# Decay attention and a gated feed-forward: more of the first batch in float32 on TensorE, and unit scales from shared parts

## The chip, the cores and the metric

The kernel runs on one core of one Trainium2 chip. The time is the device time of one execution, in microseconds (us), median over several executions. A core has five engines that run their own queues of instructions: TensorE (PE in the profile, with its weight loads as PEld), VectorE (DVE), ScalarE (ACT), GpSimd (POOL) and SyncE (SP), which here issues every DMA. An instruction waits for semaphores of other engines at the head of its own queue.

## The reference

Attention with a running decay over 8 batches of 8 heads (576 positions, 64 channels), then a feed-forward block over the 4608 tokens:

```python
scores = scale * np.matmul(q, k.transpose(0, 1, 3, 2))
cum = np.cumsum(np.log(np.clip(f, 0.0001, 1.0)), axis=-1)
decay = cum[:, :, :, None] - cum[:, :, None, :]
scores = np.where(causal, -1000000000.0, scores + decay)
attn = np.exp(scores - np.max(scores, axis=-1, keepdims=True))
attn = attn / (np.sum(attn, axis=-1, keepdims=True) + 1e-09)
x = np.matmul(attn, v)            # heads are then joined to 512 channels for each token
h = x @ w_in                      # 512 -> 2048
g = np.where(h >= 1, h, np.where(h <= -1, 0.0, (h + 1) ** 2 / 4.0))
out = g @ w_out                   # 2048 -> 512
```

Everything is float32 in and out.

## The kernel before, in words

**Attention jobs.** A job is one pair of heads of one batch. A batch is four jobs; the first batch is cut in two by rows (CUTS, L29), so jobs 0 to 3 hold its query rows 0 to 255 and jobs 4 to 7 its rows 256 to 575. There are 36 jobs, and jobs 8 to 35 are the batches 1 to 7. A job goes by row blocks r of 128 query rows (0 and 1 in jobs 0 to 3; 2, 3 and 4 in jobs 4 to 7; the last block has 64 rows, and both heads share its partitions). For each block `scores` makes q·k on PE and the decay and mask on POOL (L487, L491), into a buffer of a ring; `weights` takes the row maximum on DVE (L570), the exponential and its sum on ACT (L574), and turns the block so that keys lie on partitions. Then one matmul group per job multiplies with v, and two instructions write the result as two float16 parts, high and low, into the batch's buffer `xs[b]`.

**Two ways to turn.** Jobs below NPE (5) stay in float32: ACT scales an identity by 1/sum (L501), PE multiplies each 128x128 block by it, which turns and divides it at once (L512, L518), ACT copies the turned blocks out of PSUM (L523), and the product with v is a float32 matmul (`early_values`, L543). From job NPE on, each block is split into a high and a low float16 part (ACT L588, DVE L594), the parts are turned by DMA (L600, L603), v is split likewise (L446, L447), and the product is three float16 matmuls (`values`, L614). For jobs 6 and 7 POOL_LOW (L34) gives the low part of blocks 2 and 4 to POOL (L592), after one more ACT pass (L591). The float32 way borrows the `pr` buffers as extra score buffers and for the scaled identities: its ring has 8 score buffers, the other way's has 4.

**Weights of the feed-forward.** w_in and w_out come in 16 loads of 1 MB (L197), two to a block. Each raw load sits in a place that other data needs later (RAW, L42): slots of the weight tile itself, a spare buffer, or `xs[1]`, the buffer of batch 1's attention output. `weight_split` rounds and splits a load on DVE (L206, L209, L212), takes norms (ACT L216, PE L128), and makes the two float16 parts (ACT L221; POOL L223 and L226 for w_in, DVE L228 for w_out). CONVERT (L38) says which jobs the eight blocks are put beside.

**Units.** A unit is 256 tokens by one weight block: 24 or 48 matmuls into PSUM tile `ph` (L656; two such buffers, also used by L512 and L518), two ACT and one DVE instruction for the gate (L665, L666, L667), two for its float16 parts (L669, L670), and 12 matmuls into `po` (L684). There are 144. Those of the first 256 tokens run in three weight groups (EARLY, L36), as the weights come in. A unit needs scales: `moe_scales` makes them in 14 DVE instructions (L287 to L312), once for each of the three early groups, then once a batch, 11 times in all.

**Order.** The code lists the work in the order above, but the launch (L846) lets the framework order each engine's queue by a simulated timeline, so the order on the chip differs from that of the text.

Of the kernel before, what the change touches and what calls it, by code (L numbers as in the profile page):

```python
# [8 lines left out]
F32 = mybir.dt.float32  # L9
F16 = mybir.dt.float16  # L10
I32 = mybir.dt.int32
AF = mybir.ActivationFunctionType
ALU = mybir.AluOpType
AX = mybir.AxisListType

P = 128
EVEN_EXP = 0x7F000000
HALF_BIAS = 0x1FC00000
LOW = 2.0 ** -40
HIGH = 2.0 ** 60  # L20
MASKED = -3.0e38
# [6 lines left out]

CUTS = {0: ((0, 2), (2, 5))}  # L29

NPE = 5
NQK = 12

POOL_LOW = {6: (2, 4), 7: (2, 4)}  # L34

EARLY = ((0, 0, 3), (0, 3, 6), (0, 6, 8))  # L36

# [8 lines left out]
def kernel(  # L46
# [100 lines left out]
    def decay_sums():  # L147
        fl = early
        nb = B * H
        nc.sync.dma_start(fl[0:nb, 0:S], f.rearrange("b h s -> (b h) s"))  # L150
# [123 lines left out]
    early_z = const.tile([P, 5, NB], F32, name="early_z")  # L274

    class Scales:
        pass

    def moe_scales(b, first=0, last=NB - 1, early_group=False):
# [5 lines left out]
        w = early_z[:, :, blocks] if early_group else tiny.tile([P, 5, NB], F32, name="z")  # L285
        z.t, z.h, z.u, z.r, z.o = (w[:, i] for i in range(5))
        nc.vector.tensor_scalar(out=z.t, in0=sw[:, 0, blocks], scalar1=sv[:, b:b + 1], scalar2=None, op0=ALU.mult)  # L287
# [6 lines left out]
        nc.vector.reciprocal(z.u, z.h)
        nc.vector.tensor_scalar(out=z.u, in0=z.u, scalar1=0.5, scalar2=None, op0=ALU.mult)
        nc.vector.tensor_scalar(out=z.h, in0=z.h, scalar1=0.5, scalar2=None, op0=ALU.mult)
        gm = tiny.tile([P, 1], F32, name="gm", bufs=2)
        sm = tiny.tile([P, 1], F32, name="sm", bufs=2)
        nc.vector.tensor_reduce(out=gm, in_=mp[:, 0, blocks], axis=AX.X, op=ALU.max)
        nc.vector.tensor_reduce(out=sm, in_=mp[:, 1, blocks], axis=AX.X, op=ALU.max)  # L300
        nc.vector.tensor_scalar(
            out=gm, in0=gm, scalar1=mv[:, b:b + 1], scalar2=OVER * 1.001 * DM ** 0.5, op0=ALU.mult, op1=ALU.mult
        )
        nc.vector.tensor_scalar(out=gm, in0=gm, scalar1=1.0, scalar2=None, op0=ALU.max)
        even_pow2(gm, gm)
        z.osc = z.o[:, 0:1]
        nc.vector.tensor_scalar(
            out=z.osc, in0=gm, scalar1=sm, scalar2=4.0 / PSC, op0=ALU.mult, op1=ALU.mult
        )
        nc.vector.tensor_tensor(out=z.r, in0=z.t, in1=sw[:, 1, blocks], op=ALU.mult)  # L310
        nc.vector.tensor_scalar(out=z.r, in0=z.r, scalar1=z.osc, scalar2=None, op0=ALU.mult)
        nc.vector.reciprocal(z.r, z.r)  # L312
        return z


# [240 lines left out]
    def weights(w, r):  # L556

        if r == w.r0:
            w.pT = one.tile([P, NT5, 2, 2, S], F16, name="pT")
        nh = 2 if r < LAST else 1  # L560
        wid = min(P * (r + 1), S)
        sds = w.sds[r]
        if w.p >= NPE:
            pr = one.tile([P, PRN[r]], F16, name=f"pr{r}")
            pr = pr.rearrange("p (t l h e) -> p t l h e", t=r + 1, l=2, h=nh)
        nm = tiny.tile([P, 2], F32, name="nm", bufs=8)
        sm = tiny.tile([P, 2], F32, name="sm2", bufs=8)
        for i, (sd, sp) in enumerate(sds):
            a = sd[:, 0:wid]
            nc.vector.tensor_tensor_reduce(  # L570
                out=a, in0=sp[:, 0:wid], in1=a, scale=w.nalpha, scalar=BIG, op0=ALU.add, op1=ALU.min,
                accum_out=nm[:, i:i + 1],
            )
            nc.scalar.activation(a, a, AF.Exp, bias=nm[:, i:i + 1], scale=-1.0, accum_out=sm[:, i:i + 1])  # L574
        rc = tiny.tile([P, 2], F32, name="rc", bufs=8)
        if w.p < NPE:
            nc.vector.tensor_scalar(out=rc[:, 0:nh], in0=sm[:, 0:nh], scalar1=1e-9, scalar2=None, op0=ALU.add)
            nc.vector.reciprocal(rc[:, 0:nh], rc[:, 0:nh])
            turn_rows(w, r, [sd for sd, sp in sds], rc, diags[turn[2] % len(diags)])
            turn[2] += 1  # L580
            return
        nc.vector.tensor_scalar(
            out=rc[:, 0:nh], in0=sm[:, 0:nh], scalar1=1e-9, scalar2=1.0 / PSC, op0=ALU.add, op1=ALU.mult
        )
        nc.vector.reciprocal(rc[:, 0:nh], rc[:, 0:nh])  # L585
        for i, (sd, sp) in enumerate(sds):
            a = sd[:, 0:(r + 1) * P].rearrange("p (t e) -> p t e", e=P)
            nc.scalar.activation(pr[:, :, 0, i, :], a, AF.Copy, scale=rc[:, i:i + 1])  # L588
            mode = POOL_LOW.get(w.p, ())
            if r in mode:  # L590
                nc.scalar.activation(a, a, AF.Copy, scale=rc[:, i:i + 1])  # L591
                nc.gpsimd.tensor_tensor(out=pr[:, :, 1, i, :], in0=a, in1=pr[:, :, 0, i, :], op=ALU.subtract)  # L592
            else:
                nc.vector.scalar_tensor_tensor(  # L594
                    out=pr[:, :, 1, i, :], in0=a, scalar=rc[:, i:i + 1], in1=pr[:, :, 0, i, :],
                    op0=ALU.mult, op1=ALU.subtract,
                )
# [253 lines left out]
```

## Time and profile before

| | |
|---|---|
| median of 3 runs | 1129.2 us (1126.28 to 1130.91) |
| the profiled execution: its time, and its span from first to last instruction | 1127.8 us, 1126.0 us |
| mean granted TensorE clock | 0.956 |
| busy: DVE, ACT, POOL | 803.2 us (71%), 787.8 us (70%), 427.5 us (38%) |
| DMA: mean rate, packets under 512 B | 135 GB/s, 383968 of 408281 |

Busy times of the engines overlap: they don't add up to the span. A share over the whole span mixes three stages. Up to about 300 us the weights come in and the first two batches start; then attention jobs and units run side by side; from about 960 us on only units are left.

### The profile page before, as it was taken

The numbers are of one execution on the slowest core, as the hardware profiler recorded it, in microseconds if no ns is written. First come the engines' busy times: TensorE is split into PE (matmuls) and PEld (weight loads), VectorE is DVE, ScalarE is ACT, GpSimd is POOL, SyncE is SP. The second block draws the span as 40 slices with busy tenths as digits, with TensorE's granted clock in tenths as the row PEclk, the third lists the DMA queues.
The fourth block names the chain that finished last, engine by engine and source line by source line (L and its number), as shares of the span: only waits on it lengthen the run. The fifth ranks groups of instructions, "written<-read, shape, count | busy, mean of one in ns | idle before, by whom it ended". The sixth has DMA issues, their size and how long they took to land.

```text
span 1126.0 us, 24406 instructions
## 1 busy us (share of the span) xinstructions
PE 1020.5 (91%) x8809; PEld 662.4 (59%) x8809; DVE 803.2 (71%) x2102; ACT 787.8 (70%) x1638; POOL 427.5 (38%) x679
## 2 busy tenths in 40 slices
PE   4656667799799999999999999999999999999998
PEld 3433434556566666666766666666665666677665
DVE  5769989879788887877667668787888887332222
ACT  4567776768877887787677767787878887443443
POOL 4466775424563544444223324444444452000000
PEclk9758888899999999999999999999999999999999
DMA  7967876657886656565543656566676552300000
GB/s 221 288 177 199 225 205 176 149 126 174 202 164 156 156 132 159 140 149 149 112 100 78 155 115 153 142 151 138 161 142 149 122 123 60 78 20 2 19 20 19
DMA packets 408281, 152.18 MB, mean 135 GB/s; under 512 B 383968, under 2 KB 384992, under 8 KB 408160
## 3 DMA queue, kind: packets, MB, share of 16 engines
q1 hardware_dynamic: 408160, 150.63, 56.4%
q8 instruction: 69, 1.13, 0.4%
q14 instruction: 52, 0.43, 0.1%
HBM read 75.64 MB, written 9.58 MB: 76 GB/s over the span
## 4 chain that ended last, share of the span: by engine, by line
PE 34%; ACT 15%; DVE 7%; DMA 3%; SPq 3%; issue 2%; ACTq 0%; DVEq 0%
PE po L684 15%; PE ph L656 15%; ACT sdr L574 4%; DMA qk<-in_k_dram 3%; ACT pr L588 2%; SPq L349 2%; ACT g L669 2%; PE s L614 2%; ACT u L666 2%; PE s L481 2%; DVE qs L415 2%; ACT u L665 1%; DVE u L667 1%; DVE pr L594 1%; ACT bits L396 1%
## 5 line engine op out<-in xcount | busy, mean ns | idle before, releaser
L656 PE MATMUL ph<-x,place 128*128 128x256 f16 (+3 forms) x4608 | 417.9, 249 | 19.3 <-DVE u L667 16.5
L684 PE MATMUL po<-place,g 128*128 128x512 f16 x1728 | 404.8, 383 | 7.9 <-ACT g L669 6.7
L656 PEld LDWEIGHTS <-place 128*128 128x128 f16 x4608 | 355.7, 99 | 82.0 <-issue 33.9
L684 PEld LDWEIGHTS <-g 128*128 128x128 f16 x1728 | 167.2, 100 | 184.5 <-ACT g L669 9.2
L487 POOL TENSOR_SCALAR sdr<-ck,nsig,cqs 128x128 f32<-128x128 f32 (+1 forms) x192 | 157.1, 822 | 163.5 <-DVE pr L594 152.4
L667 DVE SCALAR_TENSOR_TENSOR u<-ph,z,u 128x512 f32<-128x512 f32 x136 | 101.7, 748 | 117.4 <-ACT u L666 115.4
L574 ACT ACTIVATE sdr<-sdr,nm 128x384 f32<-128x384 f32 (+1 forms) x248 | 137.2, 554 | 50.4 <-DVE nm L570 47.1
L665 ACT ACTIVATE u<-ph,z 128x512 f32<-128x512 f32 x136 | 104.3, 767 | 83.9 <-PE ph L656 83.8
L481 PE MATMUL s<-qkT 64*64 64x512 f16 (+11 forms) x1056 | 119.9, 341 | 33.8 <-DVE nm L570 20.8
L594 DVE SCALAR_TENSOR_TENSOR pr<-sdr,rc,pr 128x384 f16<-128x384 f32 (+2 forms) x232 | 132.6, 605 | 21.3 <-ACT pr L588 19.7
L670 DVE SCALAR_TENSOR_TENSOR g<-u,z,g 128x512 f16<-128x512 f32 x136 | 105.0, 772 | 53.4 <-ACT g L669 52.8
L669 ACT ACTIVATE g<-u,z 128x512 f16<-128x512 f32 x136 | 97.3, 716 | 62.9 <-DVE u L667 62.9
L487 POOL TENSOR_SCALAR sd<-ck,nsig,cqs 64x576 f32<-64x576 f32 x48 | 44.1, 919 | 235.8 <-issue 141.3
L588 ACT ACTIVATE pr<-sdr,rc 128x384 f16<-128x384 f32 (+1 forms) x236 | 119.1, 554 | 6.0 <-DVE rc L585 2.3
L570 DVE CUSTOM_DVE_ANT_0 sdr<-s,sdr,nalpha 128x128 f32<-128x128 f32 (+1 forms) x192 | 97.2, 545 | 19.0 <-POOL sdr L491 11.8
L491 POOL TENSOR_SCALAR_AFFINE_SELECT sdr<-sdr 128x128 f32<-128x128 f32 x248 | 88.9, 369 | 9.9
L666 ACT ACTIVATE u<-u 128x512 f32<-128x512 f32 x144 | 89.7, 623 | 2.3
L614 PE MATMUL s<-pT,vs 128*64 128x320 f16 (+3 forms) x1098 | 71.5, 282 | 7.2 <-DMA pT<-pr 6.0
L487 POOL TENSOR_SCALAR sdr<-ck,cq 128x384 f32<-128x384 f32 (+3 forms) x56 | 45.5, 813 | 65.5 <-DVE pr L594 28.1
L614 PEld LDWEIGHTS <-vs 128*64 128x64 f16 x1098 | 49.6, 112 | 31.2 <-issue 12.7
L396 ACT ACTIVATE bits<-qk 128x640 f16<-128x640 f32 x48 | 35.2, 734 | 44.7 <-DMA qk<-in_q_dram 25.5
L481 PEld LDWEIGHTS <-qkT 64*128 64x128 f16 (+1 forms) x864 | 32.8, 99 | 56.6 <-issue 39.0
(154 smaller groups left out, 992.5 us busy)
## 6 DMA issues: line engine op xcount, KB each, us to landing
ck<-cum_d SPq DMA_DIRECT2D x64, 288.0 KB, 3.8
out_dram<-ot SPq DMA_DIRECT2D x36, 256.0 KB, 2.0
qk<-in_k_dram SPq DMA_DIRECT2D x64, 128.0 KB, 2.7
vst<-in_v_dram SPq DMA_DIRECT2D x28, 288.0 KB, 3.1
v<-in_v_dram SPq DMA_DIRECT2D x62, 128.0 KB, 2.6
qk<-in_q_dram SPq DMA_DIRECT2D x56, 128.0 KB, 2.7
place<-in_moe_w_in_dram SPq DMA_DIRECT2D x6, 1024.0 KB, 7.1
place<-in_moe_w_out_dram SPq DMA_DIRECT2D x5, 1024.0 KB, 7.5
```

Source lines behind the costliest of these rows:

```text
L481: nc.tensor.matmul(sds[h % len(sds)][1][p0:p1, c0:c1], lhsT=a[rows, q0 - w.s0:q0 - w.s0 + p1 - p0], rhs=b[rows, c0:c1], start=(i == 0), st ...
L487: nc.gpsimd.tensor_scalar(out=sd[p0:p1, 0:wid], in0=w.ck[h][p0:p1, 0:wid], scalar1=w.nsig if w.p < NQK else w.nsig[p0:p1], scalar2=w.cqs[p ...
L574: nc.scalar.activation(a, a, AF.Exp, bias=nm[:, i:i + 1], scale=-1.0, accum_out=sm[:, i:i + 1])
L588: nc.scalar.activation(pr[:, :, 0, i, :], a, AF.Copy, scale=rc[:, i:i + 1])
L594: nc.vector.scalar_tensor_tensor(out=pr[:, :, 1, i, :], in0=a, scalar=rc[:, i:i + 1], in1=pr[:, :, 0, i, :], op0=ALU.mult, op1=ALU.subtract,)
L614: nc.tensor.matmul(av[64 * h:64 * h + 64, at + s0:at + s1], lhsT=w.vs[:, vl, h, t, :], rhs=w.pT[:, t, pl, h, s0:s1], start=(t == 0 and pi ...
L656: nc.tensor.matmul(ph[:, fi, a0:a1], lhsT=wi[fb][:, wl, t, fi * P:(fi + 1) * P], rhs=xs[b][:, t, xl, s0:s0 + a1 - a0], start=(fi == 0 and ...
L665: nc.scalar.activation(u, h, AF.Relu, scale=z.u[:, i:i + 1], bias=z.h[:, i:i + 1])
L666: nc.scalar.activation(u, u, AF.Square)
L667: nc.vector.scalar_tensor_tensor(out=u, in0=h, scalar=z.t[:, i:i + 1], in1=u, op0=ALU.max, op1=ALU.min)
L669: nc.scalar.activation(g[:, 0], u, AF.Copy, scale=z.r[:, i:i + 1])
L684: nc.tensor.matmul(po[ch][i], lhsT=g[:, gl, fi * TC + i * P:fi * TC + (i + 1) * P], rhs=wo[fb][:, wl, fi, :], start=(first and fi == 0 and ...
```

## The change

NPE goes from 5 to 8: jobs 5, 6 and 7 turn in float32 as jobs 0 to 4 do. POOL_LOW and its branch go. The unit scales are rebuilt: three DVE instructions for each early weight group (`block_scales`) and three more for each batch (in `value_scale`) make parts that `moe_scales` combines. Each of its 11 calls then has five DVE instructions and four on POOL; the maxima are reduced once for each range of blocks. Each call takes its tiles from the small rotating pool. The load of f is written as the first line of work instead of standing in `decay_sums` behind the loads of job 0.

```diff
-NPE = 5
+NPE = 8
-POOL_LOW = {6: (2, 4), 7: (2, 4)}
...
-        nc.sync.dma_start(fl[0:nb, 0:S], f.rearrange("b h s -> (b h) s"))
...
+        root, inverse = roots[:, 0, b:b + 1], roots[:, 1, b:b + 1]
+        nc.vector.tensor_scalar(
+            out=root.bitcast(I32), in0=pv[:, b:b + 1].bitcast(I32), scalar1=1, scalar2=None, op0=ALU.logical_shift_right
+        )
+        nc.vector.tensor_scalar(out=root, in0=root, scalar1=2.0 ** 126, scalar2=None, op0=ALU.mult)
+        nc.vector.reciprocal(inverse, root)
...
+    def block_scales(first, last):
+        blocks = slice(first, last + 1)
+        nc.vector.tensor_scalar(
+            out=block[:, 0, blocks].bitcast(I32), in0=mp[:, 0, blocks].bitcast(I32), scalar1=1, scalar2=None,
+            op0=ALU.logical_shift_right,
+        )
+        nc.vector.reciprocal(block[:, 1, blocks], block[:, 0, blocks])
+        nc.vector.tensor_tensor(out=block[:, 2, blocks], in0=mp[:, 0, blocks], in1=mp[:, 1, blocks], op=ALU.mult)
...
+        if (first, last) not in tops:
+            top = tops[first, last] = highest[:, len(tops)]
+            nc.vector.tensor_reduce(out=top, in_=mp[:, :, blocks], axis=AX.X, op=ALU.max)
...
+        nc.gpsimd.tensor_scalar(out=z.t, in0=sw[:, 0, blocks], scalar1=sv[:, b:b + 1], **one_)
+        nc.gpsimd.tensor_scalar(
+            out=z.h, in0=block[:, 1, blocks], scalar1=roots[:, 1, b:b + 1], scalar2=0.25, op0=ALU.mult, op1=ALU.mult
+        )
+        nc.gpsimd.tensor_scalar(out=z.u, in0=block[:, 0, blocks], scalar1=roots[:, 0, b:b + 1], **one_)
...
+        nc.vector.reciprocal(inverse, z.osc)
+        nc.gpsimd.tensor_scalar(
+            out=z.r, in0=block[:, 2, blocks], scalar1=pv[:, b:b + 1], scalar2=inverse, op0=ALU.mult, op1=ALU.mult
+        )
...
-            mode = POOL_LOW.get(w.p, ())
-            if r in mode:
-                nc.scalar.activation(a, a, AF.Copy, scale=rc[:, i:i + 1])
-                nc.gpsimd.tensor_tensor(out=pr[:, :, 1, i, :], in0=a, in1=pr[:, :, 0, i, :], op=ALU.subtract)
-            else:
-                nc.vector.scalar_tensor_tensor(
+            nc.vector.scalar_tensor_tensor(
...
             if nw == end:
-                z = moe_scales(0, first, end - 1, True)
+                block_scales(first, end - 1)
+                z = moe_scales(0, first, end - 1)
...
+    nc.sync.dma_start(early[0:B * H, 0:S], f.rearrange("b h s -> (b h) s"))
     pairs = [load(0)]
     decay_sums()
```

More of the change, by code (lines that the diff above doesn't have):

```diff
@@ L17 @@
 EVEN_EXP = 0x7F000000
-HALF_BIAS = 0x1FC00000
 LOW = 2.0 ** -40
@@ L272, in value_scale, with moe_scales @@
         scale_of(sv[:, b:b + 1], pv[:, b:b + 1], m)
-    early_z = const.tile([P, 5, NB], F32, name="early_z")
+        root, inverse = roots[:, 0, b:b + 1], roots[:, 1, b:b + 1]
[4 more added lines that the diff above has]
+        nc.vector.reciprocal(inverse, root)
+    roots = const.tile([P, 2, B], F32, name="roots")
+    block = const.tile([P, 3, NB], F32, name="block")
+    tops = {}
+    highest = const.tile([P, 4, 2], F32, name="highest")
     class Scales:
         pass
-    def moe_scales(b, first=0, last=NB - 1, early_group=False):
+    def block_scales(first, last):
[6 more added lines that the diff above has]
+        nc.vector.tensor_tensor(out=block[:, 2, blocks], in0=mp[:, 0, blocks], in1=mp[:, 1, blocks], op=ALU.mult)
+    def moe_scales(b, first=0, last=NB - 1):
         z = Scales()
@@ L284, in moe_scales @@
         n = last + 1 - first
-        w = early_z[:, :, blocks] if early_group else tiny.tile([P, 5, NB], F32, name="z")
-        z.t, z.h, z.u, z.r, z.o = (w[:, i] for i in range(5))
-        nc.vector.tensor_scalar(out=z.t, in0=sw[:, 0, blocks], scalar1=sv[:, b:b + 1], scalar2=None, op0=ALU.mult)
+        if (first, last) not in tops:
+            top = tops[first, last] = highest[:, len(tops)]
+            nc.vector.tensor_reduce(out=top, in_=mp[:, :, blocks], axis=AX.X, op=ALU.max)
+        top = tops[first, last]
@@ new lines, in moe_scales @@
+        w = tiny.tile([P, 4, NB], F32, name="z")[:, :, 0:n]
+        z.t, z.h, z.u, z.r = (w[:, i] for i in range(4))
+        osc = tiny.tile([P, 3], F32, name="osc")
+        z.osc, gm, inverse = (osc[:, i:i + 1] for i in range(3))
+        one_ = dict(scalar2=1.0, op0=ALU.mult, op1=ALU.mult)
+        nc.gpsimd.tensor_scalar(out=z.t, in0=sw[:, 0, blocks], scalar1=sv[:, b:b + 1], **one_)
+        nc.gpsimd.tensor_scalar(
+            out=z.h, in0=block[:, 1, blocks], scalar1=roots[:, 1, b:b + 1], scalar2=0.25, op0=ALU.mult, op1=ALU.mult
+        )
@@ L288, in moe_scales @@
+        nc.gpsimd.tensor_scalar(out=z.u, in0=block[:, 0, blocks], scalar1=roots[:, 0, b:b + 1], **one_)
+        bound = OVER * 1.001 * DM ** 0.5
         nc.vector.tensor_scalar(
-            out=z.h.bitcast(I32), in0=z.t.bitcast(I32), scalar1=1, scalar2=None, op0=ALU.logical_shift_right
+            out=gm, in0=top[:, 0:1], scalar1=mv[:, b:b + 1], scalar2=1.0 / bound, op0=ALU.mult, op1=ALU.max
         )
+        nc.vector.tensor_scalar(out=gm, in0=gm, scalar1=bound, scalar2=None, op0=ALU.mult)
@@ L291, in moe_scales @@
+        even_pow2(gm, gm)
         nc.vector.tensor_scalar(
-            out=z.h.bitcast(I32), in0=z.h.bitcast(I32), scalar1=HALF_BIAS, scalar2=None, op0=ALU.add
+            out=z.osc, in0=gm, scalar1=top[:, 1:2], scalar2=4.0 / PSC, op0=ALU.mult, op1=ALU.mult
         )
[L294 to L302, printed above, removed]
-        )
-        nc.vector.tensor_scalar(out=gm, in0=gm, scalar1=1.0, scalar2=None, op0=ALU.max)
-        even_pow2(gm, gm)
@@ L306, in moe_scales @@
[L306 to L312, printed above, removed]
+        nc.vector.reciprocal(inverse, z.osc)
+        nc.gpsimd.tensor_scalar(
+            out=z.r, in0=block[:, 2, blocks], scalar1=pv[:, b:b + 1], scalar2=inverse, op0=ALU.mult, op1=ALU.mult
+        )
@@ L588, in weights @@
             nc.scalar.activation(pr[:, :, 0, i, :], a, AF.Copy, scale=rc[:, i:i + 1])
-            mode = POOL_LOW.get(w.p, ())
-            if r in mode:
-                nc.scalar.activation(a, a, AF.Copy, scale=rc[:, i:i + 1])
-                nc.gpsimd.tensor_tensor(out=pr[:, :, 1, i, :], in0=a, in1=pr[:, :, 0, i, :], op=ALU.subtract)
-            else:
[L594 to L597, printed above, removed]
+            nc.vector.scalar_tensor_tensor(
+                out=pr[:, :, 1, i, :], in0=a, scalar=rc[:, i:i + 1], in1=pr[:, :, 0, i, :],
+                op0=ALU.mult, op1=ALU.subtract,
+            )
         dst = w.pT.rearrange("p t l h s -> p (t l h) s")[:, 0:4 * (r + 1), P * r:min(P * (r + 1), S)]
```

## The prediction, made before the changed kernel ran

> **What bounds the kernel now.** I read the page's busy times first, then the same by stretches of the span.
>
> ```profile
> PE 1020.5 (91%) x8809; PEld 662.4 (59%) x8809; DVE 803.2 (71%) x2102; ACT 787.8 (70%) x1638; POOL 427.5 (38%) x679
> ```
>
> The windows view, without its heading; after the length of the stretch come the busy times of PE, PEld, DVE, ACT and POOL, then the granted PE clock and the DMA share:
>
> ```profile
> 60.00:100.00 40.00, 24.04 (x132) 15.06 (x132) 27.45 (x73) 28.08 (x58) 26.67 (x30) 0.76 0.66 179
> 100.00:150.00 50.00, 33.36 (x200) 18.36 (x200) 49.86 (x99) 37.55 (x69) 36.46 (x39) 0.80 0.84 209
> 150.00:220.00 70.00, 50.19 (x313) 29.47 (x314) 62.82 (x188) 50.33 (x110) 38.75 (x54) 0.80 0.74 180
> 220.00:300.00 80.00, 71.89 (x560) 43.16 (x559) 64.45 (x194) 57.42 (x126) 31.84 (x55) 0.97 0.72 162
> 300.00:960.00 660.00, 645.13 (x6140) 423.66 (x6138) 512.63 (x1393) 513.38 (x1096) 264.59 (x446) 1.00 0.61 137
> ```
>
> PE is idle for 1126.0 - 1020.5 = 105.5 us. From 300 to 960 us it idles only 660 - 645.1 = 14.9 us. So the kernel ends when PE has worked through a fixed amount, and what can be won lies in the first 300 us: PE idles 16.0 us of 60 to 100, 16.6 of 100 to 150 and 19.8 of 150 to 220. A start that is shorter by X moves all that follows by X; a start that is cheaper on another engine and no shorter brings nothing.
>
> What holds the start? From 100 to 150 us DVE is busy 49.9 of 50 us, and no other engine is over 37.6. The order of events is in the timelines of SP's queue, DVE, POOL and ACT:
>
> ```profile
> 99.25 0.37 SPq L197 DMA_DIRECT2D place<-in_moe_w_in_dram  x1
> ...
> 106.98 2.62 DVE L206 TENSOR_SCALAR bits<-place 128x1024 int32<-128x1024 int32 x1
> ...
> 149.19 2.95 POOL L226 TENSOR_TENSOR place<-place 128x1024 f16<-128x1024 f32 x1
> ...
> 152.17 0.38 SPq L197 DMA_DIRECT2D place<-in_moe_w_out_dram  x1
> ...
> 181.50 0.37 SPq L197 DMA_DIRECT2D x<-in_moe_w_out_dram  x1
> ...
> 205.55 2.10 POOL L226 TENSOR_TENSOR place<-x,place 128x1024 f16<-128x1024 f32 x1
> ...
> 207.81 0.63 ACT L623 ACTIVATE x<-s 128x576 f16<-128x576 f32 x1
> ```
>
> The load issued at 99.25 is first touched by DVE at 106.98. Behind that block in the same DVE queue comes the next; its POOL part ends at 149.19 + 2.95 = 152.14, and a load into its slot goes out at 152.17: the slot had to come free. The last load leaves at 181.50. Its block's POOL instruction ends at 207.65, and ACT writes batch 1's first output at 207.81, since that buffer had held raw weights. So a chain of load, DVE rounding, norms, ACT and POOL parts, load again runs from 99 to 208 us and gates batch 1's values. Work taken out of the DVE queue between 107 and 152 us shortens it; work that DVE does elsewhere does not.
>
> **The change, part by part.** *DVE, removed.* The groups of DVE instructions between 88 and 152 us (count, then busy us and mean ns):
>
> ```profile
> L594 DVE SCALAR_TENSOR_TENSOR pr<-sdr,rc,pr 128x512 f16<-128x512 f32 (+1 forms) x8 | 8.2, 1036 | 0.0
> ...
> L447 DVE SCALAR_TENSOR_TENSOR vs<-v,sv,vs 128x640 f16<-128x640 f32 x2 | 2.2, 1087 | 0.0
> ...
> L594 DVE SCALAR_TENSOR_TENSOR pr<-sd,rc,pr 128x640 f16<-128x640 f32 x1 | 0.9, 859 | 0.0
> ...
> L287 DVE TENSOR_SCALAR early_z<-sw,sv 128x3 f32<-128x3 f32 x2 | 0.5, 240 | 0.0
> ...
> L312 DVE RECIPROCAL early_z<-early_z 128x3 f32<-128x3 f32 x2 | 0.3, 164 | 0.0
> ```
>
> The low parts of jobs 5 to 7 cost 8.2 + 0.9 us and two of their v splits 2.2 us: 11.3 us. The two early calls of the scales are 14 groups, of which the first and the last by program line stand here; at the mean of the two, 0.2 us, 28 instructions are 5.6 us. They become two times 9 (five, three parts, one maximum); at the 0.164 us of the last row that is 3.0 us, so 2.6 go. In all 13.9 us leave a queue that is full. Only what is queued behind the landed load counts for the chain:
>
> ```profile
> 117.12 1.07 DVE L594 SCALAR_TENSOR_TENSOR pr<-sdr,rc,pr 128x512 f16<-128x512 f32 x1
> ...
> 143.89 0.74 DVE L594 SCALAR_TENSOR_TENSOR pr<-sdr,rc,pr 128x512 f16<-128x512 f32 x1
> ```
>
> These are the first and the last of four L594 between 106.98 and 149.19: 4 x 1.036 = 4.1 us, with one v split 1.1 and half of the scales 1.3, together 6.5 us. Bounds: 0 (if other waits of the chain fill the hole) and all 13.9.
>
> *ACT and POOL.* Groups of the same stretch, then those of job 4, the one job of that shape which is turned in float32 already (62 to 100 us):
>
> ```profile
> L588 ACT ACTIVATE pr<-sdr,rc 128x384 f16<-128x384 f32 (+1 forms) x12 | 7.3, 661 | 1.7 <-issue 1.3 <-ACT sdr L574 0.4
> L592 POOL TENSOR_TENSOR pr<-sdr,pr 128x384 f16<-128x384 f32 x4 | 4.3, 1078 | 10.1 <-ACT sdr L591 10.0
> L588 ACT ACTIVATE pr<-sd,rc 128x640 f16<-128x640 f32 x3 | 2.5, 819 | 0.2 <-DMA ck<-cum_d 0.2
> L591 ACT ACTIVATE sdr<-sdr,rc 128x384 f32<-128x384 f32 x4 | 2.3, 598 | 0.0
> ```
>
> ```profile
> L523 ACT ACTIVATE pT<-ph 128x512 f32<-128x512 f32 (+2 forms) x6 | 2.8, 497 | 0.0
> ...
> L501 ACT ACTIVATE pr<-ident,rc 128x128 f32<-128x128 f32 x5 | 1.7, 394 | 0.0
> ```
>
> ACT loses 7.3 + 2.5 + 2.3 = 12.1 us and two smaller groups, and gains 3 x (2.8 + 1.7) = 13.5 us. I call that even. But the new copies L523 wait for PE and for the last job's product to be done with the turned tile, and behind them in ACT's queue stand the weights' L216 and L221; I charge 1 us (0 if the framework puts them late, 3 if each of the three jobs pays one). POOL loses six L592 (four in the row) and their 10 us of blocked queue, behind which job 7's scores stood. What is late next is the score buffer; the ring is 8 deep there instead of 4, so I expect no new wait, and count no gain.
>
> *DMA and SP.* Twelve transposes leave SP's queue (four a job), and with them their waits in front of loads.
>
> ```profile
> place<-in_moe_w_in_dram SPq DMA_DIRECT2D x6, 1024.0 KB, 7.1
> ...
> x<-in_moe_w_out_dram SPq DMA_DIRECT2D x3, 1024.0 KB, 5.5
> pT<-pr SPq DMA_TRANSPOSE x180, 3.3
> ```
>
> Loads into the weight tile, most of them among the transposes, land in a median of 7.1 us, those into the spare buffers in 5.5. Two loads of the chain fall into the relieved stretch: 2 x 1.6 = 3.2 us at most, 0 at least (the gap may be the slot and not the traffic). I take 2, nearer to the dear end, since the load of 99.25 came to its first use after 7.7 us.
>
> *PE, added.* Timeline of job 4's float32 work, then the float16 product of two of the jobs that change (29 of 30 matmuls each):
>
> ```profile
> 75.22 2.93 PE L512 MATMUL ph<-pr,sdr 128*128 128x128 f32 x12
> ...
> 79.77 2.05 PE L512 MATMUL ph<-pr,sdr 128*128 128x128 f32 x16
> ...
> 85.33 1.52 PE L518 MATMUL ph<-pr,sd 128*128 128x128 f32 x10
> ...
> 88.34 2.16 PE L543 MATMUL s<-pT,vs 128*64 128x320 f32 x16
> ...
> 117.68 3.04 PE L614 MATMUL s<-pT,vs 128*64 128x320 f16 x29
> ...
> 136.10 1.75 PE L614 MATMUL s<-pT,vs 128*64 128x320 f16 x29
> ```
>
> Float32 costs 2.93 + 2.05 + 1.52 + 2.16 = 8.7 us (and 4 small ones), float16 3.04 or 1.75, mean 2.4: net 6.3 a job, 19 us for three. The sum holds it at zero because 32.6 us of PE idle time lie between 60 and 150 us, and 32.6 - 19 - 8 still leaves some 6 us. If that cover is gone, the surplus shows one for one (a rival below). The first two rows give the price from both sides: 0.244 us a matmul, and 0.128. With all 38 matmuls at the one or the other, and the dearer or cheaper product on the other side, the net is 3 x 8.4 = 25 or 3 x 5.3 = 16 us.
> The Trainium skill (TensorE: Matmul & The Clock Gate, Part 1) says that PE runs at half its clock until about 3.4 us of sustained activity release it. The two spacings agree, a factor of 1.9. By that rule denser PE work in this stage (clock 0.76 and 0.80) keeps the cheaper price, and the net would be 16 us.
>
> *Scales after 200 us.* Three calls (the last early group, batch 0, batch 1) crowd DVE there, and PE waits once for a DVE read of `ph`:
>
> ```profile
> 211.20 5.07 PE L656 MATMUL ph<-x,place 128*128 128x256 f16 x24 [4.10 <-DVE u L667]
> ```
>
> 42 instructions become some 20, so I take 2 us of these 4.10 (bounds 0 and 4.1). Later calls count nothing:
>
> ```profile
> 258.35 0.22 DVE L287 TENSOR_SCALAR z<-sw,sv 128x8 f32<-128x8 f32 x1
> ```
>
> ```profile
> 0.00:258.35 258.35, 9.25 (x12) 0.82 0.75 195
> ```
>
> Batch 2's scales are begun at 258.35 us. By then 12 first instructions of units (L665 on ACT) have run, and the 33rd is the first that needs them. The three new DVE instructions a batch hide in the same slack.
>
> *f first.* It is first already:
>
> ```profile
> 0.75 0.59 SPq L150 DMA_DIRECT2D x<-in_f_dram  x1
> ```
>
> The framework had put it ahead of job 0's loads: zero, both ways.
>
> *Order.* The framework orders queues anew. I can't work that out; it widens the range by 5 us on each side, a third of the 14.9 us that PE idles in its long stage, and is in no term.
>
> **Sum.** 6.5 (DVE in the chain) + 2 (loads) - 1 (ACT's queue) + 2 (after 200) = 9.5 us. Against the profiled execution of 1127.8 us (span 1126.0 and 1.8 around it) that is 1118.3. The median shown is 1.4 higher, so I forecast **1119.5 us**.
>
> **The rivals.** *Hidden* (0.23). The chain is loads and hand-overs more than DVE: from 152.17 to 181.50 a turn takes 29 us though DVE is less full there (62.8 of 70). Then the hole closes, and 0 to 4 us are left: 1125 to 1129. For it: each step waits for another engine. Against it: DVE's idle share is nil exactly where blocks 4 and 5 are rounded.
> *PE becomes the bound* (0.16), the side on which it gets slower. Between 60 and 150 us PE has 57.4 us of work; with 19 more it has 76.4. PE idled 28% of 150 to 220 us because it waits in order for ACT and DVE, and float32 adds such waits: each of 18 PSUM groups is copied by ACT before the next but one may start, in buffers that units hold as well. At 28% idle the stage lasts 76.4 / 0.717 = 106.6 us, not 90: 1146. It decides from 76.4 / 90 = 85% busy; below that share reached, the change loses. Against it: 220 to 300 us runs at 90%.
> *The scales wait in POOL's queue* (0.07). The three early groups need them at once, and a call may stand behind an L226 of 2.95 us, with the unit's ACT instruction and the next block's L221 behind it: 3 x 2.95 = 8.9 us, so the gain is given back: 1128. The Trainium skill (GPSIMD Engine Reference, 4.1 Engine selection) advises VectorE, not GpSimd, for elementwise work on a tile, which speaks against this part.
> *More than that* (0.06). All 13.9 us of DVE, 3.2 of loads and 4.1 count: 21 us, 1108.
> That f changes nothing is the one part that doesn't do what it says; it is in the forecast.
>
> **How the numbers follow.** My forecast, 6 to 15 us faster, has 0.48. A measurement of this kernel tells about 0.5%, 5.6 us, from no change. Faster: 0.48 + 0.06 = 0.54. Same: hidden and POOL's queue, 0.30. Slower: 0.16. The range goes from 1108 less 4 for order, 1104, to 1129 plus 5, 1134; it leaves out PE as the bound and a little at the low end, 0.18.
>
> **What would show it.** Right: no L592, no DMA transposes before batch 1, DVE under 90% in a stretch of 50 us from 95 us on; the ACT write of batch 1's first output some 8 us before 207.81; PE busy in all some 15 to 20 us more, and less idle time before 300 us by more than that. Wrong: that write still near 207 (hidden), or later with PE's clock near full and waits of L512 for ACT or of `ph` for DVE (PE as the bound); units' L665 waiting for POOL (its queue). If PE idles 10 us more or less after 300 us, the new order did it, and not these steps.

## The result, and the profile after

| | median | ratio to before | 95% interval |
|---|---|---|---|
| before | 1127.74 us (1124.22 to 1130.91, 4 runs) | | |
| after | 1156.9 us (1152.48 to 1160.38, 4 runs) | 1.0261 | 1.0232 to 1.0291 |

The change makes the kernel 2.6% slower. The forecast was 1119.5 us with a range up to 1134: wrong in its sign, and the time lies outside the range. Line numbers in rows of a changed kernel are those of its own text, so L501 is there the decay row on POOL and no longer the identity on ACT.

The page of the changed kernel has this line of busy times:

```profile
PE 1047.1 (90%) x8893; PEld 681.5 (59%) x8893; DVE 777.6 (67%) x2017; ACT 785.3 (68%) x1647; POOL 425.5 (37%) x717
```

Its windows (columns as in the prediction: length, then the busy times of PE, PEld, DVE, ACT and POOL, the granted clock, the DMA share, GB/s):

```profile
60.00:100.00 40.00, 31.81 (x155) 19.22 (x156) 24.20 (x61) 27.63 (x59) 33.12 (x48) 0.68 0.68 174
100.00:150.00 50.00, 34.55 (x198) 23.87 (x198) 38.81 (x85) 32.18 (x62) 18.90 (x24) 0.80 0.53 161
150.00:220.00 70.00, 56.90 (x347) 35.99 (x344) 48.70 (x136) 43.73 (x93) 30.31 (x47) 0.88 0.49 131
220.00:300.00 80.00, 70.88 (x539) 41.38 (x538) 64.21 (x194) 61.18 (x139) 38.81 (x70) 0.94 0.84 172
300.00:960.00 660.00, 626.29 (x5879) 407.48 (x5875) 492.85 (x1326) 496.36 (x1064) 267.61 (x460) 0.99 0.66 135
```

DVE is relieved as forecast (38.81 of 50 us from 100 to 150, not 49.86). But in the long stage from 300 to 960 us, of which the prediction said that PE only works through a fixed amount there, PE now idles 660 - 626.3 = 33.7 us, where it had idled 14.9. The kernel loses most where none of its edited lines does much. The long stage shows why in the DMA issues. Before (last column: median us from issue to landing; the row of `pT` stands in the prediction, 3.3):

```profile
qkT<-qs SPq DMA_TRANSPOSE x24, 4.6
```

After:

```profile
pT<-pr SPq DMA_TRANSPOSE x168, 3.6
...
qkT<-qs SPq DMA_TRANSPOSE x24, 5.1
```

The same transposes of the same tiles land later. They stand in SP's queue ahead of the loads of q and k, and ACT, which squares q and k, waits for those. The costliest groups have ACT's row before (after the last bar: idle time of ACT ahead of this group, and the share of it that the load of q ended):

```profile
L396 ACT ACTIVATE bits<-qk 128x640 f16<-128x640 f32 x48 | 35.2, 734 | 44.7 <-DMA qk<-in_q_dram 25.5
```

and after:

```profile
L410 ACT ACTIVATE bits<-qk 128x640 f16<-128x640 f32 x48 | 35.2, 734 | 71.7 <-DMA qk<-in_q_dram 56.1
```

The instruction itself takes 734 ns both times; its wait for q has grown by 30.6 us.

### The profile page after: what moved, and what is told of

It reads as the page before. It is cut to its first block, busy times and chain, and to the rows that moved or that the text cites. A ratio compares the mean times of both kernels' runs of the same rounds, so it can differ in the third digit from the quotient of the medians.

```text
span 1158.5 us, 24534 instructions
## 1 busy us (share of the span) xinstructions
PE 1047.1 (90%) x8893; PEld 681.5 (59%) x8893; DVE 777.6 (67%) x2017; ACT 785.3 (68%) x1647; POOL 425.5 (37%) x717
## 4 chain that ended last, share of the span: by engine, by line
PE 31%; ACT 19%; DVE 9%; DMA 5%; SPq 3%; issue 2%; ACTq 0%; DVEq 0%
PE po L693 14%; PE ph L665 14%; ACT sdr L588 5%; DMA qk<-in_k_dram 3%; ACT pr L602 3%; ACT g L678 2%; SPq L363 2%; ACT u L675 2%; DVE qs L429 2%; DVE pr L603 2%; ACT u L674 2%; PE s L623 1%; PE s L495 1%; ACT bits L410 1%; DVE u L676 1%
## 5 line engine op out<-in xcount | busy, mean ns | idle before, releaser
L501 POOL TENSOR_SCALAR sdr<-ck,nsig,cqs 128x128 f32<-128x128 f32 (+1 forms) x192 | 159.1, 833 | 148.2 <-DVE pr L603 140.8
L676 DVE SCALAR_TENSOR_TENSOR u<-ph,z,u 128x512 f32<-128x512 f32 x144 | 107.6, 748 | 137.8 <-ACT u L675 134.4
L674 ACT ACTIVATE u<-ph,z 128x512 f32<-128x512 f32 x144 | 110.4, 767 | 87.0 <-PE ph L665 84.2
L588 ACT ACTIVATE sdr<-sdr,nm 128x128 f32<-128x128 f32 (+1 forms) x240 | 131.8, 550 | 47.3 <-DVE nm L584 47.0
L679 DVE SCALAR_TENSOR_TENSOR g<-u,z,g 128x512 f16<-128x512 f32 x144 | 110.7, 769 | 52.1 <-ACT g L678 51.5
L678 ACT ACTIVATE g<-u,z 128x512 f16<-128x512 f32 x144 | 103.0, 715 | 60.5 <-DVE u L676 60.3
L501 POOL TENSOR_SCALAR sd<-ck,nsig,cqs 64x576 f32<-64x576 f32 x48 | 44.4, 925 | 262.0 <-issue 136.5
L603 DVE SCALAR_TENSOR_TENSOR pr<-sdr,rc,pr 128x384 f16<-128x384 f32 (+2 forms) x224 | 122.4, 581 | 19.6 <-ACT pr L602 18.1
L602 ACT ACTIVATE pr<-sdr,rc 128x384 f16<-128x384 f32 (+2 forms) x224 | 112.0, 548 | 2.5 <-DVE rc L599 1.3
L505 POOL TENSOR_SCALAR_AFFINE_SELECT sdr<-sdr 128x128 f32<-128x128 f32 x240 | 79.3, 343 | 9.0
L623 PE MATMUL s<-pT,vs 128*64 128x64 f16 (+3 forms) x1008 | 64.4, 279 | 6.3 <-DVE nm L584 3.6
L501 POOL TENSOR_SCALAR sdr<-ck,cq 128x128 f32<-128x128 f32 (+3 forms) x48 | 34.6, 721 | 69.5 <-DVE pr L603 18.9
```

The source lines that it names most:

```text
L501: nc.gpsimd.tensor_scalar(out=sd[p0:p1, 0:wid], in0=w.ck[h][p0:p1, 0:wid], scalar1=w.nsig if w.p < NQK else w.nsig[p0:p1], scalar2=w.cqs[p ...
L603: nc.vector.scalar_tensor_tensor(out=pr[:, :, 1, i, :], in0=a, scalar=rc[:, i:i + 1], in1=pr[:, :, 0, i, :], op0=ALU.mult, op1=ALU.subtract,)
L623: nc.tensor.matmul(av[64 * h:64 * h + 64, at + s0:at + s1], lhsT=w.vs[:, vl, h, t, :], rhs=w.pT[:, t, pl, h, s0:s1], start=(t == 0 and pi ...
L674: nc.scalar.activation(u, h, AF.Relu, scale=z.u[:, i:i + 1], bias=z.h[:, i:i + 1])
L676: nc.vector.scalar_tensor_tensor(out=u, in0=h, scalar=z.t[:, i:i + 1], in1=u, op0=ALU.max, op1=ALU.min)
L678: nc.scalar.activation(g[:, 0], u, AF.Copy, scale=z.r[:, i:i + 1])
```

## The experiments

Ratios are to the kernel before, run beside it on the same chip, with 95% intervals. The runs stood in five groups on four chips, and the medians of the kernel before differ between the groups by up to 0.18% (1124.15 to 1126.13 us), so small differences between runs of different groups are unsure. "Tiles where they lay" means that the large tiles have the addresses that they had in the kernel before.

| run | what | ratio | interval |
|---|---|---|---|
| e1 | eight jobs alone | 1.0066 | 1.0043 to 1.0088 |
| e2 | new scales and f alone | 1.0359 | 1.0341 to 1.0377 |
| e3 | before, tiles 32 bytes further | 1.0254 | 1.0232 to 1.0276 |
| e4 | the change, tiles where they lay | 1.0014 | 0.9998 to 1.0030 |
| e5 | as e2, tiles where they lay | 1.0078 | 1.0055 to 1.0101 |
| e6 | the change, tiles 64 bytes further | 1.0262 | 1.0244 to 1.0280 |
| e7 | before, transposes' sources off by 32 | 1.0262 | 1.0242 to 1.0282 |
| e8 | before, transposes' destinations off by 32 | 1.0016 | 1.0004 to 1.0029 |
| e9 | the change, tiles 128 bytes further | 1.0237 | 1.0210 to 1.0264 |
| e10 | as e4, value loads into two buffers | 1.0085 | 1.0070 to 1.0100 |
| e11 | as e4, late weights' low halves on DVE | 0.9932 | 0.9916 to 0.9948 |
| e12 | as e4, one weight group a job later | 0.9997 | 0.9983 to 1.0011 |
| e13 | as e4, six jobs and not eight | 1.0060 | 1.0034 to 1.0087 |
| e14 | before, late weights' low halves on DVE | 0.9968 | 0.9948 to 0.9988 |
| e15 | e1, late weights' low halves on DVE | 0.9907 | 0.9875 to 0.9938 |

**The two parts apart (e1, e2).** The third part needs no run: with f first alone, the program built holds the same instructions in the same order on every queue.

```diff
-NPE = 5
+NPE = 8
```

> The kernel before with NPE = 8 as its only edit: jobs 5 to 7 turn in float32, scales and f as before. Theory A (the turning delays the end of batch 0: one turned tile, two ph buffers shared with units, score buffers held until PE has turned them): nearly all of the loss is here, 1148 to 1160 us, and batch 0's last output near 205 us instead of 165. Theory B (the scales in POOL's queue cost the time): within 5 us of before, 1123 to 1133. Theory C (the new order of the queues alone, no cause in either part): a loss of 10 to 20 us in this run and in the run of the scales alone.

The second run is the changed kernel with five jobs and POOL_LOW put back.

> The changed kernel with NPE = 5 and the POOL branch of jobs 6 and 7 put back: only the new scales and the load of f stay of the change. Theory A: 1120 to 1131 us, batch 0's last output near 165 us. Theory B: 1145 to 1158, with units' first ACT instruction waiting for POOL in the early groups. Theory C: 1135 to 1150.

The eight jobs cost 0.66%, the scales 3.59%, and both together 2.61%: the loss comes with the scales. None of the three theories fits: e1's 1131.88 us lie in the range of theory B, though batch 0's last output came late, at 196.6 us, as theory A had it, and e2's 1165.29 us lie above every range named. And the instructions of the scales don't account for it. On POOL they are 44 of some 0.4 us, spread over 800 us, and the trace of e2 shows the kernel falling behind by another 24 us from job 13 to job 35, some 1.1 us a job, in jobs without a scale call too. On PE, stretches with the same matmuls in the same order ran later because ACT had waited for a load of q. What is different for every transpose of the kernel? The tables. `early_z` (5 x 8 float32, 160 bytes a partition) went; `roots` (64), `block` (96) and `highest` (32) came, 192 bytes. They are declared behind the weight tile and ahead of the other large tiles, so each of these moved by 32 bytes:

```
                     before    after
pr0 (source)         146688    146720
qs  (source)         184832    184864
pT  (destination)    159488    159520
qkT (destination)    189952    189984
```

These are byte addresses in a partition; the left column holds multiples of 256.

**Only the addresses (e3 to e6).** Each of these holds the same instructions in the same order on every queue as the kernel that it is made from. e3, from the kernel before:

```diff
-    early_z = const.tile([P, 5, NB], F32, name="early_z")
+    early_z = const.tile([P, 6, NB], F32, name="early_z")
```

> The kernel before with one table, early_z, 32 bytes longer and never filled there: every instruction and every queue stays as it is, and all tiles declared behind the table (the sources and destinations of the DMA transposes among them) begin 32 bytes further, as they do in the changed kernel. Addresses theory (the changed kernel's scale tables take 192 bytes a partition where the old one took 160, and the DMA transposes got slower by it): the qkT transposes' median from issue to landing goes from 4.6 us to 5.1 to 5.4, that of pT from 3.3 to 3.6 to 3.8, the queues' share rises from 56.4% to about 60%, and the time is 1.02 to 1.035 of before (1148 to 1165 us). Instructions theory (the scales' own instructions, their engine and the order they bring cost the time): 1.000, within 0.3%, transposes at 4.6 and 3.3 us.

e4, from the changed kernel, and e5, the same edit in e2:

```diff
-    highest = const.tile([P, 4, 2], F32, name="highest")
+    highest = tiny.tile([P, 4, 2], F32, name="highest", bufs=1)
```

> The changed kernel with its smallest new table, highest (32 bytes), taken from the last pool, so that all large tiles lie again where they lay before; every queue holds the same instructions in the same order. Addresses theory: transposes back at 4.6 and 3.3 us, and the time falls by 2% to 2.6%, to 0.995 to 1.007 of before (1122 to 1136 us): the scales cost nothing, and what is left is the part with eight jobs, 1.0066 alone. Instructions theory: unchanged, 1.026 (1.023 to 1.029).

> The new scales and f alone (five jobs turned in float32, as before) with the tiles where they lay before. It ran at 1.0359 with the tiles 32 bytes further. Addresses theory: 0.995 to 1.005 of before. Instructions theory: still 1.036.

e6, from the changed kernel:

```diff
-    highest = const.tile([P, 4, 2], F32, name="highest")
+    highest = const.tile([P, 8, 2], F32, name="highest")
```

> The changed kernel with the table highest 32 bytes longer instead: the large tiles lie 64 bytes behind where they lay before (multiples of 64 again, no longer of 256); the same instructions in the same order. Addresses theory with a boundary at 64 bytes: as with the tiles where they lay, 0.995 to 1.007. Addresses theory with a boundary at 128 or 256 bytes: still slow, 1.015 to 1.03, transposes at 5.1 and 3.6 us. Instructions theory: 1.026.

32 unused bytes slow the kernel before by 2.54% (e3), and 32 bytes less take the loss out of the changed one (e4, 1.0014); e5 ended a little above its line, at 1.0078, and 64 bytes are as bad as 32 (e6). The instructions theory falls. How 32 bytes cost 28 us can be followed at one place, since the order is the same. SP's queue before (start, length, what):

```profile
694.50 2.60 SPq L420 DMA_TRANSPOSE qkT<-qs  x1
697.15 0.57 SPq L349 DMA_DIRECT2D qk<-in_q_dram  x1
```

and in e3:

```profile
709.09 3.55 SPq L420 DMA_TRANSPOSE qkT<-qs  x1
712.69 0.57 SPq L349 DMA_DIRECT2D qk<-in_q_dram  x1
```

The transpose holds SP's queue 0.95 us longer, and the loads of q behind it leave that much later. ACT's next square before, with its idle time and what ended it in brackets:

```profile
700.20 0.74 ACT L396 ACTIVATE bits<-qk 128x640 f16<-128x640 f32 x1 [1.47 <-DMA qk<-in_q_dram]
```

and in e3:

```profile
716.77 0.74 ACT L396 ACTIVATE bits<-qk 128x640 f16<-128x640 f32 x1 [4.20 <-DMA qk<-in_q_dram]
```

ACT sits 4.20 us at the head of its queue, with the units' and the softmax's instructions behind it, and PE gets its turn late (e3; before, there is no wait at these two):

```profile
728.01 0.35 PE L128 MATMUL ph<-m2q,ones 128*128 128x2 f32 x2 [0.93 <-DVE u L667]
728.78 0.61 PE L684 MATMUL po<-place,g 128*128 128x512 f16 x2 [0.41 <-ACT g L669]
```

Over the kernel, e3's page, and its windows of the first 300 us and of the long stage:

```profile
PE 1032.0 (90%) x8809; PEld 667.1 (58%) x8809; DVE 801.9 (70%) x2102; ACT 787.9 (69%) x1638; POOL 423.1 (37%) x679
```

```profile
0.00:300.00 300.00, 218.61 (x1354) 131.01 (x1354) 239.99 (x637) 202.08 (x433) 159.74 (x233) 0.83 0.79 192
300.00:960.00 660.00, 628.11 (x5936) 411.32 (x5937) 499.08 (x1359) 498.28 (x1066) 259.06 (x438) 0.99 0.67 135
```

e3's span is 1149.0 us, 23.0 over that of before, and all of it lies behind the first 300 us, in which both get through nearly the same number of matmuls (1354, and 1365 before). Behind 300 us PE idles 849.0 - 813.4 = 35.6 us, against 826.0 - 807.4 = 18.6 before: 17.0 us more. The other 6.0 us are PE's busy time. Its mean granted clock was 0.950 and not 0.956, but e8 below has 0.951 and loses next to nothing, so the runs don't say what the clock has to do with these 6.0 us.

**Source or destination, and which boundary (e7 to e9).** e8 has pads in the tile pool between sources and destinations; e7 shifts everything back by 32 bytes besides.

```diff
+    one.tile([P, 4, NT5 * P], F16, name="qs")
+    one.tile([P, 8], F32, name="gap")
```

```diff
-    mv = const.tile([P, B], F32, name="mv")
+    mv = tiny.tile([P, B], F32, name="mv", bufs=1)
```

The first diff stands behind the declaration of the `pr` tiles and is e8; both together are e7, whose sources begin 32 bytes short of a multiple of 256.

> The kernel before, laid out so that the sources of the DMA transposes (pr, qs) lie 32 bytes off their old multiples of 256, and their destinations (pT, qkT) on multiples of 256; the destinations of the q, k and v loads lie 32 bytes off too, those of the decay rows do not. Every queue holds the same instructions in the same order. If the source decides (rows of 256 bytes that then straddle two blocks of 256): transposes at 3.6 to 3.8 and 5.1 to 5.4 us and 1.02 to 1.03 of before. If the destination decides: 1.000, within 0.4%, with 3.3 and 4.6 us.

> The mirror image: sources pr and qs on multiples of 256, destinations pT and qkT 32 bytes off, with the decay rows and the value tiles declared behind them. Source decides: 1.000, within 0.4%, 3.3 and 4.6 us. Destination decides: 1.02 to 1.03, 3.6 to 3.8 and 5.1 to 5.4 us. Each half of it: both runs at about 1.012.

e9 makes `highest` 128 bytes long ([P, 16, 2]).

> The changed kernel with the large tiles 128 bytes behind their old place (it had 32: 1.0261; 64: 1.0262; 0: 1.0014). Boundary at 128 bytes: 0.998 to 1.005. Boundary at 256 bytes: 1.02 to 1.028, with qkT transposes at 5.1 us.

e7's issues:

```profile
pT<-pr SPq DMA_TRANSPOSE x180, 3.8
...
qkT<-qs SPq DMA_TRANSPOSE x24, 5.2
```

e8's:

```profile
pT<-pr SPq DMA_TRANSPOSE x180, 3.3
...
qkT<-qs SPq DMA_TRANSPOSE x24, 4.7
```

The source decides, almost alone: 1.0262 with the sources off, 1.0016 with the destinations off. e7 moves the targets of the q, k and v loads and the score buffers too, but a load of q stays at 2.7 us. In e7 DVE, ACT and POOL are busy about as long as before (802.7, 787.6 and 424.2 us, against 803.2, 787.8 and 427.5), and the units' matmuls of the last stage take 273 and 379 ns as before. At 128 bytes the loss is still there (1.0237), so of the boundaries tried only 256 is left. The sharper sign is the time for which such a transpose holds SP's queue: over the 24 of `qkT` the median is 2.6 to 2.8 us in each of the eleven traces with sources on multiples of 256, and 3.3 to 3.5 in the six others. The time to landing depends on other traffic too: e13 has 5.1 us with its sources on multiples of 256. A row of a 128 x 128 half-precision block is 256 bytes, so a source at a multiple of 256 fills whole blocks, and any other straddles two. The Trainium skill (DMA: Bandwidth & Descriptors, How a descriptor splits into AXI transactions) says that a transaction must start from a multiple of 256 bytes; a row of 256 bytes that starts elsewhere then needs two and not one. That fits: 3.3 to 3.5 us of SP's queue at 32, 64 and 128 bytes alike speaks for the count of transactions and not for the bytes fetched for nothing. That this is the mechanism inside the DMA engine is argued, not shown.

**Where the forecast gain went (e10 to e15).** With equal addresses 9.5 us of gain were forecast, and e4 shows none. The first 300 us of before:

```profile
0.00:300.00 300.00, 213.11 (x1365) 128.89 (x1366) 243.61 (x648) 205.07 (x444) 162.91 (x233) 0.84 0.76 194
```

and of e4:

```profile
0.00:300.00 300.00, 223.68 (x1457) 140.23 (x1458) 219.65 (x588) 201.59 (x450) 156.77 (x248) 0.88 0.69 183
```

PE is 10.6 us busier, so its idle time there fell by 10.6 us and not by more. What is late now can be read in e4's timelines. PE:

```profile
124.84 1.16 PE L526 MATMUL ph<-pr,sdr 128*128 128x128 f32 x8 [1.29 <-DVE mp L126]
...
140.81 0.59 PE L125 MATMUL ph<-m2w,ones 128*128 128x2 f32 x2 [7.59 <-ACT place L212]
```

ACT:

```profile
138.35 1.22 ACT L212 ACTIVATE place<-place 128x1024 f16<-128x1024 f32 x1 [5.10 <-POOL place L222]
```

POOL:

```profile
125.44 1.25 POOL L501 TENSOR_SCALAR sdr<-ck,cq 128x128 f32<-128x128 f32 x2 [12.96 <-PE ph L526]
...
132.64 2.64 POOL L219 TENSOR_SCALAR place<-place,sw 128x1024 f32<-128x1024 f32 x1
135.36 2.96 POOL L222 TENSOR_TENSOR place<-place 128x1024 f16<-128x1024 f32 x1
```

Read it from the bottom. POOL's decay row for the next job (L501) needs a score buffer that PE's turning (L526) still reads, and waits 12.96 us. Behind it in POOL's queue stand the two instructions for a weight's low half (L219, L222), behind these the square sum on ACT (L212, 5.10 us of wait), and behind that the norm on PE (L125), for which PE idles 7.59 us with job 6's remaining turning behind it. A second suspect was SP's queue, where loads of batch 1's values wait for one buffer. e10:

```diff
-            vpart[0] = one.tile([P, S], F32, name="vst")
+            spare = b == 1 and i % 2
+            vpart[0] = v32.rearrange("p h t d -> p (h t d)")[:, 0:S] if spare else one.tile([P, S], F32, name="vst")
```

> The changed kernel with its tiles where the old ones lay (1.0014 of before), and every second of batch 1's value loads into the idle tile v32 in place of vst, so that SP's queue need not hold a load until VectorE has read the one before it. In the run without this a row of six such loads takes 21.93 us of SP's queue from 122.35 us on, and the next weight load stands behind it at 145.99. If that queue eats the gain of the eight jobs: the weight load leaves by 130 us, batch 1's first output comes 5 to 15 us earlier, and the time is 0.987 to 0.996 of before. If VectorE and the turning on TensorE hold the weights anyway: 0.998 to 1.005, no more than a new order brings.

The edit did not do what it was made for. The framework ordered the queues anew, and SP's queue is held as long as before, with the weight load still behind the value loads (e10):

```profile
120.92 20.80 SPq L245 DMA_DIRECT2D vst<-in_v_dram  x5
144.00 0.38 SPq L193 DMA_DIRECT2D x<-in_moe_w_in_dram  x1
```

So 1.0085, above both lines, says nothing about the hold; what it costs stays open. The next three test the chain through POOL and its rivals. e11:

```diff
-            if j == 0:
+            if j == 0 and i < 4:
                 nc.gpsimd.tensor_scalar(
```

> The changed kernel with its tiles where the old ones lay (1.0014 of before), and the low halves of the last four weight groups' first matrix made on VectorE in one instruction, as the second matrix's are, not in two on POOL. POOL theory (decay rows wait for the turning, and the weights' halves, their square sums on ACT and their norms on TensorE wait behind them): the idle time of 7.59 us on TensorE before the norm at 140.81 shrinks to under 3 us, the last weights come 3 to 8 us earlier, and the time is 0.991 to 0.997 of before. Rival (the added TensorE work itself, or VectorE again, holds the weights): 0.999 to 1.005.

e12 has `CONVERT = {3: 2, 4: 1, 5: 2, 6: 1, 7: 1, 8: 1}` for `{3: 2, 4: 1, 5: 2, 6: 2, 7: 1}`:

> The changed kernel with its tiles where the old ones lay, and one of job 6's two weight groups made in job 7, that of job 7 in job 8. Theory that the weights' norms stand ahead of the turning in TensorE's queue and hold batch 0: batch 0's last output comes at 180 to 190 us, not 201, and the time is 0.992 to 0.999. POOL theory: the decay rows go free of the weights in job 6, but the last weights come 10 us later or more: 1.000 to 1.008.

e13 has `NPE = 6`:

> The changed kernel with its tiles where the old ones lay, but six jobs turned in float32 and not eight, the low halves of jobs 6 and 7 on VectorE and not partly on POOL. If the added TensorE work (24.7 us for three jobs) is what eats the gain: 0.992 to 0.998 of before, TensorE's busy time some 10 us less than with eight jobs. If VectorE was the bound, as the prediction had it: slower than with eight jobs, 1.004 to 1.012.

e11 gains 0.68% on before. POOL still waits for the turning, but no weight stands behind it there. Its POOL row:

```profile
125.52 1.26 POOL L501 TENSOR_SCALAR sdr<-ck,cq 128x128 f32<-128x128 f32 x2 [13.12 <-PE ph L526]
```

ACT:

```profile
133.76 1.11 ACT L212 ACTIVATE place<-place 128x1024 f16<-128x1024 f32 x1 [0.40 <-DVE place L224]
```

PE, and the first 300 us:

```profile
136.13 0.38 PE L125 MATMUL ph<-m2w,ones 128*128 128x2 f32 x2 [2.91 <-ACT place L212]
```

```profile
0.00:300.00 300.00, 233.64 (x1542) 148.37 (x1543) 226.46 (x613) 210.47 (x468) 147.72 (x252) 0.89 0.70 188
```

The square starts 4.6 us sooner, the norm 4.7, and PE fits 10.0 us more work into 300 us than in e4. In e12 batch 0's last output came at 185 us and not at 200, as the theory of PE's queue had it, but the last weight block's POOL instruction ended 7.2 us later (211.4, not 204.2), and the interval meets that of e4. Neither line was met, and the two effects may cancel. In e13 the time is 0.46% above e4's with less work on PE: had the added work eaten the gain, it should lie below. That speaks against this rival and doesn't exclude it, since the queues are ordered anew, and e5 and e10 moved by 0.7 to 0.8% with edits that relieve nothing.

Is e11's gain the change's own? e14 makes e11's edit in the kernel before, e15 in e1.

> The kernel before (five jobs, old scales, tiles where they lay) with the same edit as e11: the low halves of the last four weight groups' first matrix on VectorE. If VectorE is the bound of the first batch in the kernel before (49.9 us of 50 busy between 100 and 150 us), the edit puts some 5 us of work on the bound: 1.002 to 1.010. If POOL's queue held the weights in the kernel before too, it gains there as in e11: 0.990 to 0.997.

> Eight jobs and the weights' halves on VectorE, with the old scales (the eight jobs alone stood at 1.0066). If the halves in POOL's queue were what took the gain of the eight jobs: 0.995 to 1.000, the rest up to e11's 0.9932 being the scales' share of some 0.5%. If the new scales are needed for it: 1.003 to 1.008.

The edit alone gives 0.32% with five jobs and takes the eight jobs from 1.0066 to 0.9907, lower than its line: beside it the eight jobs gain some 0.6%, without it they lose 0.66%. Each of the two is no larger than what a new order can do; the step of 1.6% from e1 to e15 is. e14 missed its first line, but it did not load DVE as that line supposed: with four instructions more (2106, not 2102) DVE is busy 799.0 us and not 803.2, since others got shorter (below, DVE beside POOL). So e14 doesn't test whether DVE was the bound, and the edit has a second possible cause beside POOL's queue: a faster DVE. The runs don't part the two. The new scales add nothing to e15 that can be told (e11 is at 0.9932, and the intervals meet). With the scales the other runs go both ways: 1.0078 with five jobs, 1.0014 against 1.0066 with eight. So they have no fixed worth; I take what they do for new order, which is argued, not shown. e15, the eight jobs with the old scales, is the fastest of all, at 1116.53 us.

## Why the prediction was wrong, step by step

- **What bounds the kernel.** That PE works through a fixed amount and any idle time it gets is the loss was right, and it is what the loss was found by. That DVE's queue holds the first batch was at best half right: relieving it paid only together with POOL's (e15, against e1).
- **The step that failed.** The part on the scales counted instructions ("42 instructions become some 20") and let all later calls "count nothing". It did not add up the bytes of the tables that went and came: 160 to 192, and with them 2.5% (e3). The sum had no term for what moves when a table changes size; nor did any rival. What failed is that unnamed term, put at zero without a reason: the runs show some 28 us in its place (e3 against before), as longer transposes in SP's queue. The forecast named a right sign for this, "if PE idles 10 us more or less after 300 us, the new order did it": PE did idle 18.8 us more there, but e3 has that with no change of order. That attribution was wrong.
- **6.5 us from DVE's work in the chain.** DVE fell to 77.6% of the stretch, well under the 90% named. In e4 the chain did get shorter up to its last load: the load of 152.17 left at 148.22, and that of 181.50 at 169.21, 4.0 and 12.3 us sooner. But the POOL instruction of the last weight block, which ended at 207.65 us before, ended by the row below at 204.2: some 3.4 us are left of the 6.5, and batch 1's first output no longer hung on it (below). So the step was right in its direction, and its gain was lost behind the loads.

```profile
202.10 2.12 POOL L222 TENSOR_TENSOR place<-x,place 128x1024 f16<-128x1024 f32 x1
```

- **"the ring is 8 deep there instead of 4, so I expect no new wait".** The second wrong step, and by e11 and e15 the likely cause of the missing gain: the turning now reads the score buffers on PE, and POOL waits 12.96 us for it with weights behind. A deeper ring doesn't help when its reader is the engine that is late.
- **2 us from faster loads.** Mis-signed. With 12 transposes fewer, the loads into the weight tile land in a median of 7.9 us and not 7.1 (e4, the row below). Of the two in the relieved stretch, the load of 99.25 landed after 7.0 us before, and its like in e4, at 97.60, after 10.2; the next took 6.1 and 8.5.

```profile
place<-in_moe_w_in_dram SPq DMA_DIRECT2D x6, 1024.0 KB, 7.9
```

- **2 us after 200 us** from the scales: not seen; with the tiles where they lay the kernel with the scales alone is 0.78% slower (e5).
- **PE's added work at zero.** Up to 230 us the turning and the products of e4 take 22.0 us more of PE than before (29.5 more in float32, 7.5 less in float16), near the 19 forecast and not at the 16 of the cheaper price (the granted clock from 60 to 150 us only went from 0.78 to 0.81). In all PE is 10.6 us busier, with a mean granted clock of 0.967 and not 0.956, and its idle time took that up (94.0 us, not 105.5). The cover was there, and it was also all the gain there was. Much of "PE becomes the bound" did come true: from 60 to 150 us PE was 72% busy in e4, under the 85% that this rival named, the turning waited for ACT's copies, and batch 0's last output came at 200.1 us and not at 165.3. What did not follow is a later end: units fill PE meanwhile.
- **Batch 1's first output** as the gauge. It came at 223.08 us in e4 and at 216.03 in e11, after 207.81 before, and e11 is faster all the same. It doesn't gate the end; units of batch 0 are there to fill in. PE's idle time before 300 us is a better gauge, but a rough one: 86.9 us before, 76.3 in e4, 66.4 in e11, yet 75.3 in e1, which is slower than before, and 69.7 in e12, which is not faster.
- **POOL's queue for the scales** (a rival): its sign, a unit's first ACT instruction that waits for POOL, shows once in each run that has both the eight jobs and the new scales and no other edit of the work (2.8 us in the changed kernel, 3.08 in e4, the row below), and not in e5. What that wait is worth was not tested apart. The large instructions in the same queue stood behind a longer one.

```profile
198.72 0.78 ACT L674 ACTIVATE u<-ph,z 128x512 f32<-128x512 f32 x1 [3.08 <-POOL z L310]
```

- **f first**: nothing, as said. **Order**: ±5 us was too small; edits that relieve nothing moved the kernel by some 0.7 to 0.8% (e5 against before, e10 against e4). In the sum, 1118.3 and 1.4 are 1119.7 and not 1119.5, which changes nothing.

## What to carry to other kernels

When an edit adds or drops a small table, work out where the tiles declared behind it come to lie, before anything else is compared; a table of spare bytes, or a table moved to the last pool, is a test that leaves all queues as they are. When work moves to another engine, look for who reads its buffers last: that engine's queue now holds the buffer, and whatever stands behind the one who waits for it. And a gain that is missing can be sitting one queue further on: here two edits together gave 0.93% (e15), where one alone gave a third of that and the other a loss.

## What the runs showed of the hardware

- **DMA transposes are slower from a source that is off a multiple of 256 bytes**, by 32, 64 or 128 bytes alike: for 128 x 2560 a median of 3.3 to 3.5 us of the issuing queue against 2.6 to 2.8, and 5.1 to 5.4 us to landing against mostly 4.5 to 4.8. The destination doesn't matter to speak of (e8: 1.0016). The Trainium skill (DMA: Bandwidth & Descriptors, DMA Transpose (X-bar), Constraints) asks for an address that is a multiple of 32 bytes; the sources that are 32 bytes off keep to that, and cost 2.6% of this kernel (e7).
- **DVE beside POOL.** In e4 the same DVE instruction on 128 x 1024 words takes 1.31 us at 131.18, beside POOL's selects, and 3.01 us beside POOL's L222 at 135.36:

```profile
131.18 1.31 DVE L208 SCALAR_TENSOR_TENSOR x<-x,bits 128x1024 int32<-128x1024 int32 x1
...
136.39 3.01 DVE L208 SCALAR_TENSOR_TENSOR x<-x,bits 128x1024 int32<-128x1024 int32 x1
```

In e11, with POOL's two gone, the one that follows at 137.35 takes 1.23. The kernel before has such a row at 134.10, of 3.15 us beside POOL's L226, and e14 has 1.21 in its place. Part of the gain of e11, e14 and e15 may come from there; that was not tested apart.
